# Sparse attention and a mixture of experts on one core: the first expert chunk of each batch in eight plain block products instead of seven

## The chip, the cores and the metric

One NeuronCore of a Trainium2 chip runs the whole program. The metric is the device time of one execution in microseconds (us), the median over runs. The engines are TensorE (PE in the profile; matmuls into PSUM), VectorE (DVE), ScalarE (ACT), GpSimd (POOL) and SyncE (SP, which only issues DMAs here). Each works through its own instruction list in order; semaphores connect them.

## The reference

Block-sparse attention over 4 batches, 8 heads, 768 positions and head size 64, followed by four experts whose outputs are mixed with given weights:

```
scores = where(mask, q @ k.T / 8, -1e9)     # mask: neighbours, first and last block of 32, 3 sampled blocks
attn = softmax(scores) @ v                  # x = attn of all heads side by side: [3072, 512]
p = domain_probs / (domain_probs.sum(-1) + 1e-9)
for e in range(4):
    out += p[:, e:e+1] * (relu(x @ w1[e]) @ w2[e])     # w1 [512, 1024], w2 [1024, 512]
```

All inputs and outputs are float32.

## The kernel before

**Attention.** Each batch has 16 units: 4 for the first and last row block, 12 for six groups of up to four row blocks, half of the heads each. A unit goes through `S` (scores into PSUM, then mask and row minimum on DVE at L266, exponential on ACT at L269), `T` (transposes on PE, copies on ACT at L280), `A` (times v on PE at L291, division on DVE) and `X` (transposes on PE, and a copy into `xr`, the batch's tokens as 512 x 768). For batch 0 a loop of 19 rounds does `S` of unit n, `X` of n-3, `A` of n-2 and `T` of n-1, with nothing else for PE to do. The attention of batches 1 to 3 is laid between the expert work of the batch before, by estimated times (`drive`).

**Experts.** A chunk is half of an expert's hidden layer, four tiles of 128; there are 8 chunks per batch. The first layer of a chunk is done in two halves `s`. For each, w1 is a 2 x 2 block matrix (output half, k half) and the tokens are a 2 x 2 block matrix b11, b12, b21, b22 (k half, token half g of 384 tokens). The kernel before multiplies them with seven products of sums of blocks (Winograd's form of Strassen's method), in the order 2, 1, 5, 6, 3, 7, 4. The sums of weight blocks are made on DVE (L456 to L461), those of token blocks in `conversion` (L407 to L418), and the products are combined on DVE and ACT (L522 to L536).

Every operand is written as a rounded part and a remainder. The rounded part is a cast on ACT (`wo` L464 for weights, `xo` L392 for tokens, `h` L480 for w2). The remainder is a subtraction on POOL (L465, L481) or, for tokens, on DVE or POOL (L393). One product is six matmuls of 384 columns (L502): two k tiles times three pairs of parts. ReLU and its split are L509 on ACT and L510 on DVE. The second layer (`second`, L550) does three matmuls of 512 columns per step into one of three `po` banks; after the last of the four tiles, DVE adds the bank, times the token's weight, into `oacc` (L565).

**Order of the work.** Nothing is reordered after the program is written: each engine gets its instructions in the order in which the code emits them. `experts` emits first-layer products and second-layer steps so that ten products stand ahead of a batch's first step. When the last product of a batch is emitted, 18 steps remain; behind every second step from there on, `convert` emits one more piece of the next batch's token conversion. Weights run ahead too: `operands` keeps seven weight blocks ready, and `split_w2` makes the next chunk's w2 tile once the old one is used up, then asks for another load (L444). PSUM holds two attention banks `s`, one `a`, one each of `v` and `w` for first-layer products, and three `po`.

**The token weights.** `token_weights` issues the load of `probs` on SP (L620) and right behind it four DVE instructions (L621 to L624) that divide by the sums. It is called in round 9 of batch 0's loop. In round 12 the first two token blocks, which need only the first token half, are converted.

Of the kernel before, what the change touches and what calls it, by code (L numbers as in the profile page):

```python
# [8 lines left out]
F32 = mybir.dt.float32  # L9
# [8 lines left out]
P = 128  # L18
# [5 lines left out]
def attention_moe_kernel(ctx: ExitStack, tc, qb, kb, vr, sampled, sampled_t, probs, w1, w2, out):  # L24
# [38 lines left out]
    def f32(ap):  # L63
        return ap.bitcast(F32)
# [322 lines left out]

    xo = {}

    def split(n, src, eng):  # L390
        o = xo[n] = (xp if n in (1, 2) else later["x"]).tile([P, 2, KH, HS], F32R, name=f"xo{n}")
        nc.scalar.copy(o[:, 0], src)  # L392
        eng.tensor_sub(o[:, 1], src, f32(o[:, 0]))  # L393

    def token_blocks(b):
        return [xr[b][:, k * KH:(k + 1) * KH, g * HS:(g + 1) * HS] for k in range(2) for g in range(2)]

    def conversion(b):


        b11, b12, b21, b22 = (xr[b][:, k * KH:(k + 1) * KH, g * HS:(g + 1) * HS]
                              for k in range(2) for g in range(2))
        split(2, b21, nc.gpsimd)
        yield
        split(1, b11, nc.vector)
        yield
        nc.vector.tensor_sub(b11, b12, b11)  # L407
        split(5, b11, nc.vector)
        yield
        nc.vector.tensor_sub(b11, b22, b11)  # L410
        split(6, b11, nc.vector)
        yield
        split(3, b22, nc.gpsimd)
        yield
        nc.vector.tensor_sub(b12, b22, b12)
        split(7, b12, nc.vector)
        yield
        nc.vector.tensor_sub(b21, b21, b11)  # L418
        split(4, b21, nc.gpsimd)
        xr.pop(b)  # L420
        yield

    pieces = {}

    def convert(b):
        if b in pieces:
# [13 lines left out]

    def load_w2(n):
        if n < B * NCH * FT:
            r2[n] = raw.tile([P, DM], F32, name="r2")
            nc.sync.dma_start(r2[n], w2[n // FT % NCH, n % FT])  # L444

    def operands():
        for b in range(B):
            for c in range(NCH):
                r, s1 = {}, {}
                for s, n in ORDER:  # L450
                    if n == 2:
# [10 lines left out]
                    src = {1: a11, 5: s1.get(s), 2: a12, 6: a11, 3: a12, 7: a21, 4: a22}[n]  # L462
                    o = wp.tile([P, 2, KH, P], F32R, name="wo", bufs=NWO)
                    nc.scalar.copy(o[:, 0], src)  # L464
                    nc.gpsimd.tensor_sub(o[:, 1], src, f32(o[:, 0]))  # L465
                    wo[b, c, s, n] = o
                    if n == 4:
                        load_w1(b * NCH + c + 1, s)
                    yield

# [3 lines left out]
    def split_w2(n):  # L474
        if n >= B * NCH * FT:
            return
        r = r2.pop(n)
        h = wp.tile([P, DM], F32R, name="h2")
        l = wp.tile([P, DM], F32R, name="l2")
        nc.scalar.copy(h, r)  # L480
        nc.gpsimd.tensor_sub(l, r, f32(h))  # L481
# [11 lines left out]

    def first(b, c, s, n):
        ps_m, cp, hp = later["m"], later["c"], later["h"]
        w, x = wo.pop((b, c, s, n)), xo[n]

        def product(ps, fresh):
            m = 0
# [6 lines left out]
        def finish(half, g, src):  # L506
# [3 lines left out]
            nc.vector.scalar_tensor_tensor(hl, src, 0.0, f32(hh), op0=ALU.max, op1=ALU.subtract)  # L510
            hs[c, 2 * s + half, g] = (hh, hl)

        if n in (5, 2, 3):
            v = ps_m.tile([P, HS], F32, name="v", bufs=1)
            product(v, True)
        else:
            if n == 1:
                W[s] = ps_m.tile([P, HS], F32, name="w", bufs=1)
            product(W[s], n == 1)
        if n == 2:  # L520
            pt[s] = cp.tile([P, HS], F32, name="p1", bufs=1)
            nc.scalar.copy(pt[s], v)  # L522
        elif n == 1:
            nc.vector.tensor_add(pt[s], W[s], pt[s])  # L524
            finish(0, 0, pt[s])
        elif n == 5:
            zt[s] = cp.tile([P, HS], F32, name="z1", bufs=2)
            nc.scalar.copy(zt[s], v)
        elif n == 6:
            ut[s] = cp.tile([P, HS], F32, name="u1", bufs=1)  # L530
            nc.vector.tensor_add(ut[s], W[s], zt[s])
        elif n == 3:
            nc.vector.tensor_add(ut[s], v, ut[s])
            finish(0, 1, ut[s])
        elif n == 7:
            nc.vector.tensor_add(zt[s], W[s], zt[s])  # L536
            finish(1, 1, zt[s])
        else:
            finish(1, 0, W[s])
# [27 lines left out]
            nc.sync.dma_start(out[tok * P:(tok + 1) * P, :], accs.pop(tok))  # L567


    TB = NCH * (len(ORDER) * T1 + KT * FT * T2)  # L570
    OFF = 10
    NH = (5, 3)

    def experts():

        L = len(ORDER)
        for b in range(B):
            one = [(c, s, n) for c in range(NCH) for s, n in ORDER]
            two = [(c, g, f, j) for c in range(NCH) for g in (1, 0) for f in range(FT)
                   for j in range(HS // P)]  # L580
            p = q = 0
            after_first = False
            while q < len(two):

                wait = after_first and p < len(one) and one[p][2] == 4 and q < ready(p)
                if wait or p >= min(len(one), (q * NCH * L + OFF * len(two)) / len(two)):
                    second(b, *two[q])
                    q += 1
                    after_first = False
# [27 lines left out]
    psum_e = const.tile([P, NT // P], F32, name="psum_e")  # L617

    def token_weights():
        nc.sync.dma_start(pr, probs)  # L620
        nc.vector.reduce_sum(psum_e, pr, axis=AX.X)  # L621
        nc.vector.tensor_scalar(psum_e, psum_e, 1e-9, None, op0=ALU.add)
        nc.vector.reciprocal(psum_e, psum_e)
# [6 lines left out]
    with ExitStack() as only:  # L630
# [13 lines left out]
        for n in range(N + 3):  # L644
# [6 lines left out]
            if 0 <= n - 1 < N:  # L651
                us[n - 1].T(0)
                us[n - 1].T(1)
            if n == 1:
                load_q(0, 1)
                load_v(0, 1)
                copy_k(0, 1)
# [4 lines left out]
                copy_k(0, t + 2)  # L662

            if n == N - 7:
                token_weights()
                for s in range(2):
                    load_w1(0, s)
                    load_w2(s)
            if n == N - 4:
                pieces[0] = conversion(0)  # L670
                convert(0)
                convert(0)
            if N - 5 <= n < N + 2:
                next(weights)
            if N - 4 <= n < N:
# [14 lines left out]
    later["h"] = ctx.enter_context(tc.tile_pool(name="hp", bufs=2 * FT))  # L690
    later["c"] = ctx.enter_context(tc.tile_pool(name="cp", bufs=2))
    later["o"] = ctx.enter_context(tc.tile_pool(name="op", bufs=KT))
    convert(0)
    LEAD, TAIL = 12.0, 25.0
    for b in range(1, B):
# [77 lines left out]
```

## Time and profile before

| | us |
|---|---|
| median of 3 runs | 1327.17 (1326.28 to 1329.41) |
| profiled execution, its own time | 1327.28 |
| its span, first to last instruction | 1325.6 |
| TensorE matmul busy | 1257.2 (95%) |
| DVE, POOL, ACT busy | 763.7, 675.7, 638.2 |

The granted TensorE clock is 0.982 of full speed on average. One batch follows the next after about 319 us. A row of a timeline gives the start, the duration, engine and line, operation and tiles; in square brackets stand the idle time of that engine just before, and what ended it. PE time includes the pipeline, so the rate of matmuls is read from their starts.

### The profile page before, as it was taken

What the parts mean: (1) busy time and instruction counts of PE and PEld (TensorE: products, weight loads), DVE (VectorE), ACT (ScalarE), POOL (GpSimd) and SP (SyncE); (2) the same over time, 40 slices, a digit from 0 to 9 for tenths busy, and PEclk for the clock granted to TensorE, in tenths of its full rate; (3) what the DMA queues carried; (4) which work ended last, traced back from release to release, by engine and by line L of the source; (5) the groups of instructions that cost most, each with busy time, mean ns of one, the idle gap of its engine ahead of it and who ended that gap; (6) DMA issues with size and microseconds to landing.
All of it is one profiled execution on the core that took longest, in us unless ns stands there. A gap on an engine that the chain in (4) does not pass through costs nothing.

```text
span 1325.6 us, 31450 instructions
## 1 busy us (share of the span) xinstructions
PE 1257.2 (95%) x12238; PEld 1076.7 (81%) x12238; DVE 763.7 (58%) x1750; ACT 638.2 (48%) x1678; POOL 675.7 (51%) x872
## 2 busy tenths in 40 slices
PE   7677999999998999999999799999999989999998
PEld 4566888888887788888888688888888778888887
DVE  5476656556547666556555756556555565555553
ACT  4474455555544445555554444555554444444441
POOL 5544545555445455664644554565553464444451
PEclk9877999999999999999999999999999999999999
DMA  8833324544214233443525311443431222222211
GB/s 252 221 108 137 96 60 115 155 118 135 89 62 173 73 96 89 130 140 92 149 64 171 110 57 57 136 144 113 128 104 54 88 88 64 64 64 65 64 48 64
DMA packets 60050, 140.51 MB, mean 106 GB/s; under 512 B 7163, under 2 KB 8700, under 8 KB 59900
## 3 DMA queue, kind: packets, MB, share of 16 engines
q1 hardware_dynamic: 52816, 115.41, 28.0%
q0 software_dynamic: 7040, 23.07, 6.3%
q8 instruction: 96, 1.57, 0.5%
q14 instruction: 54, 0.44, 0.1%
q10 hardware_dynamic: 44, 0.00, 0.0%
HBM read 132.17 MB, written 6.29 MB: 104 GB/s over the span
## 4 chain that ended last, share of the span: by engine, by line
PE 84%; DVE 7%; ACT 3%; issue 2%; DMA 1%; POOL 1%; DVEq 0%; SPq 0%; ACTq 0%
PE po L550 37%; PE w L502 19%; PE v L502 14%; PE o L291 3%; PE tp L278 3%; PE s L256 2%; PE sw L325 2%; PE s L251 2%; DVE hl L510 2%; PE ow L356 1%; DVE xo L393 1%; ACT hh L509 1%; PE tw L346 1%; ACT xo L392 1%; DVE oacc L565 1%
## 5 line engine op out<-in xcount | busy, mean ns | idle before, releaser
L465 POOL TENSOR_TENSOR wo<-r,wo 128x256 fp32r<-128x256 f32 x384 | 298.9, 781 | 419.4 <-ACT wo L464 415.6
L502 PE MATMUL w<-xo,wo 128*128 128x384 f32 x1536 | 317.1, 342 | 13.1 <-DVE z L536 8.4
L550 PE MATMUL po<-h,hh 128*128 128x512 f32 x768 | 310.6, 404 | 13.6 <-DVE oacc L565 13.1
L502 PEld LDWEIGHTS w<-xo,wo 128*128 128x128 f32 x1536 | 275.8, 190 | 39.6 <-DVE z L536 9.7
L550 PE MATMUL po<-h,hl 128*128 128x512 f32 x768 | 304.9, 397 | 0.0
L550 PE MATMUL po<-l,hh 128*128 128x512 f32 x768 | 304.8, 397 | 0.0
L502 PE MATMUL v<-xo,wo 128*128 128x384 f32 x1152 | 237.6, 342 | 10.6 <-ACT p L522 7.9
L464 ACT CAST wo<-r 128x256 fp32r<-128x256 f32 x384 | 153.6, 400 | 185.7 <-DVE r L459 116.3
L502 PEld LDWEIGHTS v<-xo,wo 128*128 128x128 f32 x1152 | 206.6, 190 | 29.6 <-ACT p L522 9.2
L481 POOL TENSOR_TENSOR l<-r,h 128x512 fp32r<-128x512 f32 x128 | 168.1, 1314 | 44.7 <-ACT h L480 44.6
L550 PEld LDWEIGHTS po<-h,hh 128*128 128x128 f32 x768 | 144.8, 189 | 37.5 <-DVE oacc L565 17.2
L550 PEld LDWEIGHTS po<-h,hl 128*128 128x128 f32 x768 | 144.9, 189 | 33.9
L550 PEld LDWEIGHTS po<-l,hh 128*128 128x128 f32 x768 | 145.1, 189 | 15.2
L524 DVE TENSOR_TENSOR p<-w,p 128x384 f32<-128x384 f32 x64 | 35.7, 557 | 169.3 <-PE w L502 166.0
L565 DVE SCALAR_TENSOR_TENSOR oacc<-po,pr,oacc 128x512 f32<-128x512 f32 x168 | 120.0, 744 | 10.3 <-PE po L550 9.7
L269 ACT ACTIVATE p<-p,mx 128x256 f32<-128x256 f32 (+1 forms) x192 | 95.4, 498 | 51.9 <-DVE mx L266 51.9
L136 POOL DMA_INDIRECT v<-in_vr_dram,vidx x88 | 86.7, 985 | 54.4 <-PE o L291 23.3
L465 POOL TENSOR_TENSOR wo<-s,wo 128x256 fp32r<-128x256 f32 x64 | 48.5, 757 | 98.1 <-ACT wo L464 93.3
L266 DVE CUSTOM_DVE_ANT_1 p<-s,mask 128x256 f32<-128x256 f32 (+1 forms) x192 | 69.7, 417 | 39.9 <-PE s L256 39.4
L480 ACT CAST h<-r 128x512 fp32r<-128x512 f32 x128 | 79.1, 618 | 12.1 <-PE po L550 10.4
L509 ACT ACTIVATE hh<-p 128x384 fp32r<-128x384 f32 x64 | 33.6, 524 | 90.8 <-DVE p L524 90.7
L510 DVE SCALAR_TENSOR_TENSOR hl<-w,hh 128x384 fp32r<-128x384 f32 x64 | 35.7, 558 | 71.4 <-ACT hh L509 71.4
(113 smaller groups left out, 1472.1 us busy)
## 6 DMA issues: line engine op xcount, KB each, us to landing
r<-in_w_dram SPq DMA_DIRECT2D x64, 512.0 KB, 3.6
r<-in_w_dram SPq DMA_DIRECT2D x128, 256.0 KB, 2.6
v<-in_vr_dram SPq DMA_DIRECT2D x44, 384.0 KB, 5.4
k<-in_kb_dram SPq DMA_DIRECT2D x8, 768.0 KB, 6.2
out_dram<-oacc SPq DMA_DIRECT2D x24, 256.0 KB, 2.1
v<-in_vr_dram SPq DMA_DIRECT2D x44, 128.0 KB, 5.4
q<-in_qb_dram SPq DMA_DIRECT2D x20, 256.0 KB, 6.9
v<-in_vr_dram SPq DMA_DIRECT2D x4, 1024.0 KB, 10.0
```

What stands on the lines that cost most here:

```text
L136: nc.gpsimd.indirect_dma_start(out=v[:, i, 1], out_offset=None, in_=vr, element_offset=b * S * DM, in_offset=bass.IndirectOffsetOnAxis(ap= ...
L266: nc.vector.tensor_tensor_reduce(p.rearrange("p (a b) -> p a b", b=BLOCK), s[h][:n, i], mk, -SCALE, 3.0e38, ALU.add, ALU.min, mx[:n])
L269: nc.scalar.activation(p, p, AF.Exp, bias=mx[:n], scale=-1.0, accum_out=self.sums[:n, m:m + 1])
L464: nc.scalar.copy(o[:, 0], src)
L465: nc.gpsimd.tensor_sub(o[:, 1], src, f32(o[:, 0]))
L480: nc.scalar.copy(h, r)
L481: nc.gpsimd.tensor_sub(l, r, f32(h))
L502: nc.tensor.matmul(ps, w[:, wi, t], x[:, xi, t], start=fresh and m == 0, stop=m == 3 * KH - 1, skip_group_check=not fresh)
L509: nc.scalar.activation(hh, src, AF.Relu)
L510: nc.vector.scalar_tensor_tensor(hl, src, 0.0, f32(hh), op0=ALU.max, op1=ALU.subtract)
L550: nc.tensor.matmul(p, a[:, js], w, start=f == 0 and n == 0, stop=f == FT - 1 and n == 2)
L565: nc.vector.scalar_tensor_tensor(accs[tok], p, pe, accs[tok], op0=ALU.mult, op1=ALU.add)
```

## The change

1. For the first chunk of each batch (c = 0) the first layer is done in eight plain products per half: the output block (half, g) is w1(half, 0) times b(0, g) plus w1(half, 1) times b(1, g), both into the same PSUM bank, and is then finished by ReLU and split straight from that bank. The order of the eight output blocks is the table `FIRST`; the first three need only the first token half. The banks `v` and `w` alternate. The weights of that chunk are then the eight plain blocks, each used twice. Two weight blocks are made behind the fourth, fifth, seventh and eighth output block, none behind the others.
2. `conversion` makes the plain b12 and b22 first and the sums later, in twelve steps with a cast one step ahead of its remainder, and two more steps (the sum for product 7, into the buffer that held plain b12) behind product 15 of the first chunk.
3. Twelve products, not ten, stand ahead of a batch's first second-layer step. Chunks 1 to 7 are as before.
4. `probs` is loaded in round 3; the four DVE instructions stand in round 17, behind the last unit's `A`.
5. w2 has three raw buffers, and three loads are asked for at the start. The tile `z1` has one buffer, not two.

```diff
     def conversion(b):
-        split(2, b21, nc.gpsimd)
-        yield
-        split(1, b11, nc.vector)
-        yield
-        nc.vector.tensor_sub(b11, b12, b11)
-        split(5, b11, nc.vector)
...
+        def cast(n, src):
+            xo[n] = (xp if n in (1, 2) else later["x"]).tile([P, 2, KH, HS], F32R, name=f"xo{n}")
+            nc.scalar.copy(xo[n][:, 0], src)
+        def rest(n, src, eng):
+            eng.tensor_sub(xo[n][:, 1], src, f32(xo[n][:, 0]))
+        cast(2, b21)
+        yield
+        rest(2, b21, nc.gpsimd)
+        cast(1, b11)
+        yield
+        rest(1, b11, nc.vector)
+        yield
+        cast(7, b12)
+        yield
+        rest(7, b12, nc.vector)
+        cast(3, b22)
+        yield
+        rest(3, b22, nc.gpsimd)
         nc.vector.tensor_sub(b11, b12, b11)
-        split(5, b11, nc.vector)
-        yield
+        yield
+        cast(5, b11)
+        yield
+        rest(5, b11, nc.vector)
         nc.vector.tensor_sub(b11, b22, b11)
...
+        yield
+        cast(6, b11)
         nc.vector.tensor_sub(b12, b22, b12)
...
+        yield
+        rest(6, b11, nc.vector)
         nc.vector.tensor_sub(b21, b21, b11)
+        yield
+        cast(4, b21)
+        yield
+        rest(4, b21, nc.gpsimd)
+        yield
+        cast(7, b12)
+        yield
+        rest(7, b12, nc.vector)
         xr.pop(b)
+    EARLY, PLAIN = 3, 12
+    FIRST = [((0, 0, 0), 0), ((0, 1, 0), 0), ((1, 0, 0), 0), ((0, 0, 1), 2), ((0, 1, 1), 2),
+             ((1, 1, 0), 0), ((1, 0, 1), 2), ((1, 1, 1), 2)]
+    XOF = {(0, 0): 1, (1, 0): 2, (0, 1): 7, (1, 1): 3}
...
-            r2[n] = raw.tile([P, DM], F32, name="r2")
+            r2[n] = raw.tile([P, DM], F32, name="r2", bufs=3)
...
-        load_w2(n + 2)
+        load_w2(n + 3)
...
     def first(b, c, s, n):
+        if c == 0:
+            half, k, g = n
+            w, x = wo[b, c, s, (half, k)], xo[XOF[k, g]]
...
+        if c == 0:
+            i = [item for item, _ in FIRST].index((s, half, g))
+            if k == 0:
+                W[0] = ps_m.tile([P, HS], F32, name="vw"[i % 2], bufs=1)
+            product(W[0], k == 0)
+            if k == 1:
+                finish(half, g, W.pop(0))
+                for _ in range(FIRST[i][1]):
+                    next(weights, None)
+            return
...
-            zt[s] = cp.tile([P, HS], F32, name="z1", bufs=2)
+            zt[s] = cp.tile([P, HS], F32, name="z1", bufs=1)
...
-                    if p < L:
-                        convert(b)
+                    if p < 2 * L:
+                        convert(b, PLAIN if p <= L else PLAIN + 2)
...
     def token_weights():
-        nc.sync.dma_start(pr, probs)
...
+            if n == 3:
+                nc.sync.dma_start(pr, probs)
+            if n == N + 1:
+                token_weights()
...
             if n == N - 7:
-                token_weights()
                 for s in range(2):
                     load_w1(0, s)
-                    load_w2(s)
+                for f in range(3):
+                    load_w2(f)
             if n == N - 4:
                 pieces[0] = conversion(0)
-                convert(0)
-                convert(0)
+                for _ in range(EARLY):
+                    convert(0)
```

PE, where batch 0's expert work begins behind the last attention transposes. `xo` with a number is one token operand (before, 2028 is b21, 2031 b11, 2462 the first sum). Before:

```order
L310 MATMUL x<-ident,xg 128x64 x4
L502 MATMUL v<-xo_2028,wo 128x384 x6
L502 MATMUL w<-xo_2031,wo 128x384 x6
L502 MATMUL v<-xo_2462,wo 128x384 x6
L502 MATMUL w<-xo_2477,wo 128x384 x6
L502 MATMUL v<-xo_2492,wo 128x384 x6
```

With the change (2029 is b11, 2026 b21, 2458 the plain b12, 2461 the plain b22):

```order
L310 MATMUL x<-ident,xg 128x64 x4
L537 MATMUL v<-xo_2029,wo 128x384 x6
L537 MATMUL v<-xo_2026,wo 128x384 x6
L537 MATMUL w<-xo_2029,wo 128x384 x6
L537 MATMUL w<-xo_2026,wo 128x384 x6
L537 MATMUL v<-xo_2029,wo 128x384 x6
L537 MATMUL v<-xo_2026,wo 128x384 x6
L537 MATMUL w<-xo_2458,wo 128x384 x6
```

The first product that reads anything of the second token half was the third in the list; it is now the seventh.

DVE, between the last product of batch 0 and the first ReLU of batch 1 (`xo` rows are remainders, `xr` rows sums of token blocks, `hl` the split behind a ReLU). Before:

```order
L393 TENSOR_TENSOR xo_6459<-xr,xo_6459 128x768
L565 SCALAR_TENSOR_TENSOR oacc<-po,pr,oacc 128x512 x2
L407 TENSOR_TENSOR xr<-xr 128x2x384
L393 TENSOR_TENSOR xo_6473<-xr,xo_6473 128x768
L565 SCALAR_TENSOR_TENSOR oacc<-po,pr,oacc 128x512
L410 TENSOR_TENSOR xr<-xr 128x2x384
L393 TENSOR_TENSOR xo_6486<-xr,xo_6486 128x768
L415 TENSOR_TENSOR xr<-xr 128x2x384
L393 TENSOR_TENSOR xo_6513<-xr,xo_6513 128x768
L418 TENSOR_TENSOR xr<-xr 128x2x384
L565 SCALAR_TENSOR_TENSOR oacc<-po,pr,oacc 128x512 x3
L524 TENSOR_TENSOR p_6572<-w,p_6572 128x384
```

With the change:

```order
L610 SCALAR_TENSOR_TENSOR oacc<-po,pr,oacc 128x512 x2
L402 TENSOR_TENSOR xo_6425<-xr,xo_6425 128x768
L610 SCALAR_TENSOR_TENSOR oacc<-po,pr,oacc 128x512
L402 TENSOR_TENSOR xo_6447<-xr,xo_6447 128x768
L417 TENSOR_TENSOR xr<-xr 128x2x384
L402 TENSOR_TENSOR xo_6486<-xr,xo_6486 128x768
L422 TENSOR_TENSOR xr<-xr 128x2x384
L610 SCALAR_TENSOR_TENSOR oacc<-po,pr,oacc 128x512 x2
L425 TENSOR_TENSOR xr<-xr 128x2x384
L610 SCALAR_TENSOR_TENSOR oacc<-po,pr,oacc 128x512
L402 TENSOR_TENSOR xo_6512<-xr,xo_6512 128x768
L428 TENSOR_TENSOR xr<-xr 128x2x384
```

The same eight token instructions stand there, but two `oacc` additions now come ahead of the first remainder, and the last three are spread between the sums; next behind these rows is `hl`.

ACT at the same place, with the change (`xo` rows are casts of tokens, `h` rows casts of w2, `hh` rows ReLU):

```order
L399 CAST xo_6447<-xr 128x768
L509 CAST h_6457<-r_6231 128x512
L399 CAST xo_6464<-xr 128x768
L509 CAST h_6477<-r_6290 128x512
L399 CAST xo_6486<-xr 128x768
L509 CAST h_6494<-r_6334 128x512
L399 CAST xo_6512<-xr 128x768
L509 CAST h_6518<-r_6461 128x512
L399 CAST xo_6535<-xr 128x768
L544 ACTIVATE hh_6543<-v 128x384
L544 ACTIVATE hh_6561<-w 128x384
```

Casts of tokens and of w2 alternate, and the last token cast, which reads the last sum of DVE's list, stands ahead of the first ReLU.

More of the change, by code (lines that the diff above doesn't have):

```diff
@@ L388, in attention_moe_kernel @@
     xo = {}
[L390 to L396, printed above, removed]
     def conversion(b):
@@ L402, in conversion, with convert @@
                               for k in range(2) for g in range(2))
-        split(2, b21, nc.gpsimd)
+        def cast(n, src):
[4 more added lines that the diff above has]
+        cast(2, b21)
         yield
-        split(1, b11, nc.vector)
+        rest(2, b21, nc.gpsimd)
+        cast(1, b11)
         yield
+        rest(1, b11, nc.vector)
[6 more added lines that the diff above has]
+        rest(3, b22, nc.gpsimd)
         nc.vector.tensor_sub(b11, b12, b11)
-        split(5, b11, nc.vector)
         yield
+        cast(5, b11)
+        yield
+        rest(5, b11, nc.vector)
         nc.vector.tensor_sub(b11, b22, b11)
-        split(6, b11, nc.vector)
         yield
-        split(3, b22, nc.gpsimd)
+        cast(6, b11)
+        nc.vector.tensor_sub(b12, b22, b12)
         yield
-        nc.vector.tensor_sub(b12, b22, b12)
-        split(7, b12, nc.vector)
+        rest(6, b11, nc.vector)
+        nc.vector.tensor_sub(b21, b21, b11)
         yield
-        nc.vector.tensor_sub(b21, b21, b11)
-        split(4, b21, nc.gpsimd)
+        cast(4, b21)
[5 more added lines that the diff above has]
+        rest(7, b12, nc.vector)
         xr.pop(b)
         yield
+    EARLY, PLAIN = 3, 12
     pieces = {}
-    def convert(b):
-        if b in pieces:
+    steps = {}
+    def convert(b, limit=PLAIN):
+        if b in pieces and steps.get(b, 0) < limit:
+            steps[b] = steps.get(b, 0) + 1
             next(pieces[b], None)
     ORDER = [(s, n) for s in range(2) for n in (2, 1, 5, 6, 3, 7, 4)]
+    FIRST = [((0, 0, 0), 0), ((0, 1, 0), 0), ((1, 0, 0), 0), ((0, 0, 1), 2), ((0, 1, 1), 2),
+             ((1, 1, 0), 0), ((1, 0, 1), 2), ((1, 1, 1), 2)]
+    XOF = {(0, 0): 1, (1, 0): 2, (0, 1): 7, (1, 1): 3}
     wo = {}
@@ L449, in operands @@
                 r, s1 = {}, {}
-                for s, n in ORDER:
-                    if n == 2:
+                plain = [(s, (i, k)) for s in range(2) for i in range(2) for k in range(2)]
+                for s, n in ORDER if c else plain:
+                    if n in (2, (0, 0)):
                         r[s] = r1.pop((b, c, s))
@@ L495, in first @@
         ps_m, cp, hp = later["m"], later["c"], later["h"]
-        w, x = wo.pop((b, c, s, n)), xo[n]
+        if c == 0:
+            half, k, g = n
+            w, x = wo[b, c, s, (half, k)], xo[XOF[k, g]]
+            if g:
+                wo.pop((b, c, s, (half, k)))
+        else:
+            w, x = wo.pop((b, c, s, n)), xo[n]
         def product(ps, fresh):
@@ L577, in experts @@
         for b in range(B):
-            one = [(c, s, n) for c in range(NCH) for s, n in ORDER]
+            one = [(0, s, (half, k, g)) for (s, half, g), _ in FIRST for k in range(2)]
+            MORE = len(one) - L
+            one += [(c, s, n) for c in range(1, NCH) for s, n in ORDER]
             two = [(c, g, f, j) for c in range(NCH) for g in (1, 0) for f in range(FT)
@@ L583, in experts @@
             while q < len(two):
-                wait = after_first and p < len(one) and one[p][2] == 4 and q < ready(p)
-                if wait or p >= min(len(one), (q * NCH * L + OFF * len(two)) / len(two)):
+                wait = after_first and p < len(one) and one[p][2] == 4 and q < ready(p - MORE)
+                if wait or p >= min(len(one), (q * NCH * L + (OFF + MORE) * len(two)) / len(two)):
                     second(b, *two[q])
```

8 lines of the change are left out of this document (5 added, 3 removed).

## The prediction

> **What bounds the kernel now.** I read the busy shares of five stretches first, then the waits of PE in the joint between two batches, then timelines of single engines there.
>
> ```profile
> 20.00:98.00 78.00, 58.64 (x1708) 45.45 (x1706) 44.74 (x182) 50.01 (x161) 37.33 (x63) 0.85 0.59 165
> 98.00:124.00 26.00, 17.54 (x67) 15.76 (x68) 17.10 (x23) 11.18 (x23) 11.55 (x11) 0.74 0.53 187
> 124.00:410.00 286.00, 284.04 (x2947) 244.40 (x2946) 163.27 (x402) 145.27 (x394) 148.45 (x199) 1.00 0.36 110
> 410.00:443.00 33.00, 25.30 (x112) 20.63 (x111) 24.10 (x29) 14.02 (x28) 19.00 (x16) 0.95 0.35 112
> 729.00:763.00 34.00, 26.31 (x118) 22.03 (x117) 24.80 (x29) 14.50 (x29) 19.91 (x17) 0.95 0.33 108
> ```
>
> The columns are the stretch, its length, busy time of PE, weight loads, DVE, ACT and POOL, then the granted clock. Within a batch (third row) PE is busy for 284 of 286 us at full clock: there every product is paid in full and no wait is left to win. What can be won lies in batch 0's attention, in its hand-over to the experts (clock 0.74), and in the three joints (the fourth and fifth rows show two).
>
> **Part 1, the token weights.** At round 9 DVE stands for a small load:
>
> ```profile
> 66.26 0.25 DVE L621 TENSOR_REDUCE psum_e<-pr 128x24 f32<-128x96 f32 x1 [6.34 <-DMA pr<-in_probs_dram]
> 67.28 0.42 DVE L266 CUSTOM_DVE_ANT_1 p<-s,mask 128x256 f32<-128x256 f32 x1
> 58.91 1.16 PE L291 MATMUL o<-v,pt 128*32 128x64 f32 x64
> 60.00 1.09 PE L278 MATMUL tp<-ident,p 128*128 128x128 f32 x8
> 70.33 1.94 PE L291 MATMUL o<-v,pt 128*32 128x64 f32 x64 [8.10 <-ACT pt L280]
> 72.20 1.97 PE L278 MATMUL tp<-ident,p 128*128 128x128 f32 x8
> ```
>
> Behind that wait queue the score rows of DVE, behind those ACT's exponentials and `pt`, and behind those PE, idle for 8.10 us. The change takes away the wait, 6.34, and the four instructions, 67.28 - 66.26 = 1.02: 7.4 us. PE then also ran at half speed: the same 64 matmuls take 1.94 instead of 1.16, the eight transposes 1.97 instead of 1.09, and the scores behind them lose about as much again, an estimate of 2.3 us in all. What is late next is the first weight block, which ACT casts in order between exponentials:
>
> ```profile
> 75.74 0.40 ACT L464 CAST wo<-r 128x256 fp32r<-128x256 f32 x1
> 60.34 0.55 SPq L444 DMA_DIRECT2D r<-in_w_dram  x1
> r<-in_w_dram SPq DMA_DIRECT2D x1, 256.0 KB, 8.9
> ```
>
> That cast would come up at 75.74 - 9.7 = 66.0. Its block was issued between `probs`, which landed at 66.26, and the load of 60.34, which landed 8.9 us later, at 69.2. So ACT waits between 0.3 and 3.2 us, and I take 1.5. Part 1 gives 7.4 + 2.3 - 1.5 = **8.2 us**, between 5 (the latest landing, part of the slow clock kept) and 9.7 (no wait). The moved load is one 0.4 us issue more on SP in round 3, ahead of later attention loads that wait for PE anyway; nothing.
>
> **Part 2, batch 0's hand-over.**
>
> ```profile
> 98.42 1.31 PE L502 MATMUL v<-xo,wo 128*128 128x384 f32 x6 [0.52 <-DVE xr L312]
> 103.55 2.12 PE L502 MATMUL v<-xo,wo 128*128 128x384 f32 x6 [2.78 <-ACT p L522]
> 122.72 0.39 PE L550 MATMUL po<-h,hh 128*128 128x512 f32 x1
> 441.02 1.20 PE L502 MATMUL v<-xo,wo 128*128 128x384 f32 x6
> 442.05 0.40 PE L550 MATMUL po<-h,hh 128*128 128x512 f32 x1
> 442.75 1.20 PE L502 MATMUL w<-xo,wo 128*128 128x384 f32 x6
> ```
>
> The first product starts as soon as the last token copy is done, at 98.4. From there to the first second-layer step at 122.7 ten products take 24.3 us, though one costs 442.05 - 441.02 = 1.03 and a step 0.70. The change puts twelve there, 12.4 us if nothing waits. But the order of ACT and DVE puts conversions ahead of ReLUs, and POOL and DVE get in each other's way:
>
> ```profile
> 419.64 1.53 POOL L481 TENSOR_TENSOR l<-r,h 128x512 fp32r<-128x512 f32 x1 [7.85 <-ACT h L480]
> 421.12 2.57 POOL L393 TENSOR_TENSOR xo<-xr,xo 128x768 fp32r<-128x768 f32 x1
> 419.94 2.04 DVE L415 TENSOR_TENSOR xr<-xr 128x768 f32<-128x768 f32 x1
> 422.89 1.62 DVE L393 TENSOR_TENSOR xo<-xr,xo 128x768 fp32r<-128x768 f32 x1 [0.90 <-ACT xo L392]
> 415.69 0.96 DVE L393 TENSOR_TENSOR xo<-xr,xo 128x768 fp32r<-128x768 f32 x1 [0.90 <-ACT xo L392]
> 409.94 1.85 POOL L393 TENSOR_TENSOR xo<-xr,xo 128x768 fp32r<-128x768 f32 x1
> 409.03 1.57 ACT L392 CAST xo<-xr 128x768 fp32r<-128x768 f32 x2
> L510 DVE SCALAR_TENSOR_TENSOR hl<-p,hh 128x384 fp32r<-128x384 f32 x14 | 11.1, 792 | 8.3 <-ACT hh L509 8.3
> L510 DVE SCALAR_TENSOR_TENSOR hl<-w,hh 128x384 fp32r<-128x384 f32 x14 | 7.8, 558 | 17.1 <-ACT hh L509 17.1
> L509 ACT ACTIVATE hh<-w 128x384 fp32r<-128x384 f32 x14 | 6.9, 491 | 7.2 <-PE w L502 7.2
> ```
>
> A token subtraction takes 0.96 alone and 2.04 beside POOL, whose own grows from 1.85 to 2.57: they end one after the other, as if they took turns. The split from PSUM (`hl<-w`) stays at 0.56, and the plain chunk has only that kind. A cast is 0.8, a ReLU 0.5.
>
> From the token copy's end: casts of plain b12 and b22 to 0.85 and 1.6, remainder of b12 on DVE to 1.9, of b22 on POOL to 3.7, first sum on DVE to 4.6, its cast to 5.4, and only then the first ReLU to 5.85 and split to 6.45. The third output block needs bank `v` back and has been due at 4.4: 2.1 us lost. Then remainder, two sums and a cast hold the second ReLU to 9.6, its split to 10.2 (1.65 lost), and a remainder, a sum and the last cast the third, to 13.4 and 14.0 (1.65 lost). The rest is free: 18.2 us, plus 0.6 since the four token-weight instructions, about 1.0 us, now stand ahead of the last token copy, plus 1.7 for one stretch of slow clock: 20.5. Part 2 gives 24.3 - 20.5 = **3.8 us**, between 0.5 (two more slow stretches) and 11.1 (nothing waits: 13.2). The two products more are paid in this.
>
> **Part 3, the three joints.**
>
> ```profile
> 408.15 0.39 PE L550 MATMUL po<-h,hh 128*128 128x512 f32 x1
> 413.32 0.50 PE L550 MATMUL po<-h,hh 128*128 128x512 f32 x1 [0.82 <-DVE oacc L565]
> 417.36 0.50 PE L550 MATMUL po<-h,hh 128*128 128x512 f32 x1 [2.38 <-DVE oacc L565]
> 429.51 1.30 PE L502 MATMUL v<-xo,wo 128*128 128x384 f32 x6 [1.23 <-ACT p L522]
> 428.46 0.62 ACT L480 CAST h<-r 128x512 fp32r<-128x512 f32 x1 [0.59 <-DMA r<-in_w_dram]
> 412.53 1.40 DVE L565 SCALAR_TENSOR_TENSOR oacc<-po,pr,oacc 128x512 f32<-128x512 f32 x2
> 415.50:419.00 3.50, 1.64 (x5) 1.30 (x6) 2.48 (x3) 0.95 (x3) 0.00 (x0) 0.83 0.21 78
> 419.00:422.50 3.50, 3.50 (x12) 2.76 (x11) 2.92 (x2) 1.77 (x4) 2.86 (x2) 0.69 0.04 6
> ```
>
> From 408.15 to 442.05 the last 18 steps and the first ten products take 33.9 us; 18 x 0.70 + 10 x 1.03 = 22.9, so 11.0 are lost. The new order ends two `oacc` additions at 412.4, the first remainder at 413.4 and the third addition at 414.05, so the steps lose only 0.4 and end at 421.15. Meanwhile DVE does a remainder and a sum to 415.95. ACT's next token cast stands behind the cast of w2's second tile, which waits for PE until 416.95, and ends at 418.35. POOL is then in turn: its token remainder to 419.0, DVE's to 419.9, POOL's `l` to 421.15, DVE's second sum to 422.0. Two additions to 423.4, the third sum to 424.35, the last addition to 425.05. POOL's last `l` goes first, to 425.6; remainder to 426.5, last sum to 427.45; last token cast to 428.3, then ReLU and split to 429.35. The third output block has been due at 421.15 + 4 x 1.03 = 425.3: 4.1 us lost. Eight products more: 429.4 + 8 x 1.03, 0.3 for restarts and 1.7 of slow clock give 439.65. The cover by w2's third buffer takes the 0.59 us DMA wait away: its load is then asked for at 417.2 and used at 422.9. A joint gains 442.05 - 439.65 = **2.4 us**, two products included, between 0.3 (POOL always first: 441.7) and 8.3 (the chain hidden: 433.75).
>
> The slow clock: after the 2.38 us gap the two stretches quoted were granted 0.83 and 0.69. That is half speed for 0.34 x 3.5 + 0.62 x 3.5 = 3.4 us, which costs 1.7; the 1.23 us gap left the clock alone. [...]
>
> **The sum.** 1327.28 - 8.2 - 3.8 - 3 x 2.4 = 1308.1; the profiled execution lies 0.1 above the median of the runs. POOL's and ACT's savings (eight weight blocks instead of 14) are off the path, as PE's 284 of 286 shows. One buffer for `z1` costs nothing:
>
> ```profile
> L510 DVE SCALAR_TENSOR_TENSOR hl<-z,hh x3: 558/558/559, 289.7 to 331.3; 128x384 fp32r<-128x384 f32 x3
> L528 ACT COPY z<-v x2: 480/480/480, 301.3 to 321.1; 128x384 f32<-128x384 f32 x2
> ```
>
> The read that frees it starts at 289.7, and the next write at 301.3, 11 us later.
>
> **Rivals.**
>
> *Conversions leave the path.* For it: ReLUs are short and DVE is busy for only 24 of 33 us in the joint. Against: the order has the last sum and cast ahead of the first ReLU. All upper ends: 1327.3 - 9.7 - 11.1 - 3 x 8.3 = 1281.6; halfway from my forecast is 1295.
>
> *Short gaps cost no clock.* The new gaps of 2.1 and 4.1 us leave PE at full speed, as the one of 1.23 us did: four times 1.7 less, 1301. Against: the 2.38 us gap. [...]
>
> *Waits are handed on.* The weights land late, the hand-over has three slow stretches, POOL goes first in each joint: 1327.3 - 5 - 0.5 - 0.9 = 1321. For it: a load of 256 KB took 8.9 us at that place, and DVE and POOL, 24.1 and 19.0 us busy and taking turns, leave a joint of 33 us little slack.
>
> *Slower: the single `z1`.* If the copy of z (28 chunks x 2 halves) had to wait for DVE's split of the other half, it would hold bank `v`; with 0.5 us each, about what the copy itself lasts, 56 x 0.5 = 28 us against 19 won: 1336. It decides from the point where that split comes 11 us later than now; nothing quoted suggests it.
>
> **How the numbers follow.** Forecast 0.60 (own range 1303 to 1315), conversions off the path 0.17, clock 0.05, handed on 0.14, slower 0.04. The range 1296 to 1319 cuts the far ends of the second and fourth. About 0.2% (2.7 us) is what a measurement can tell: faster 0.94, same 0.02, slower 0.04.
>
> **What would show it.** Right: no DVE wait on `pr`; first products at about 90 us; in the joints no PE wait for `oacc` above 1 us, and one of some 4 us before the third output block, its bank freed by `hl`; expert rows in between unchanged. Wrong: a PE wait elsewhere within a batch, a long ACT wait for `r`, or a joint without the 4 us wait.

## The result, and the profile after

The changed kernel takes 1304.41 us (median of 4 runs, 1303.35 to 1305.68); the kernel before takes 1328.29 on the same chip (4 runs, 1326.28 to 1330.34). The ratio is 0.9825, with a 95% interval of 0.9812 to 0.9838: 23.9 us less. The prediction said 1308.1, with 1303 to 1315 for the case that it held likeliest and 1296 to 1319 over all its cases. The profiled execution took 1304.3 us, its span 1302.6.

The busy shares of two stretches of the changed kernel: batch 0's hand-over to the experts, and the first joint. The columns are those of the table before.

```profile
96.00:116.00 20.00, 15.31 (x82) 14.21 (x83) 12.69 (x16) 7.79 (x15) 6.58 (x6) 1.00 0.56 202
396.00:428.00 32.00, 28.67 (x134) 25.36 (x133) 17.12 (x23) 12.46 (x23) 15.97 (x12) 0.95 0.41 135
```

Two things differ at a glance. The hand-over runs at full clock (1.00, and 0.74 before), and DVE's load in a joint has fallen from 24.1 to 17.1 us. The joint has kept its 0.95.

PE's waits from 100 us to the end in the changed kernel, with the total, how many, and the longest:

```profile
PE v L537 <- DVE hl L545: 12.2, 5, 3.1
PE po L595 <- DVE oacc L610: 2.1, 6, 0.4
PE po L595 <- DVE oacc L608: 1.7, 3, 0.6
PE w L537 <- DVE hl L545: 1.3, 1, 1.3
```

The longest of the same list in the kernel before:

```profile
PE po L550 <- DVE oacc L565: 13.1, 9, 2.4
PE w L502 <- DVE z L536: 8.4, 7, 1.9
PE v L502 <- ACT p L522: 7.9, 4, 2.8
PE w L502 <- DVE u L531: 4.4, 3, 1.6
```

With 2.1 more for z and 0.5 for `oacc` it sums to 36.4 us. These 36.4 us became 17.3. Every wait that came from combining products (p, u, z) is gone: the plain chunk, which now stands where most of those waits were, has nothing to combine. One kind took their place, and the forecast named it: the ReLU's split `hl`, 3.1 us in each joint.

The 23.0 us by which the span shrank, stretch by stretch on the same chip:

| stretch | before | after | gain | forecast |
|---|---|---|---|---|
| batch 0, to the start of the last transposes | 97.57 | 94.90 | 2.7 | 8.2 |
| from there to the first second-layer step | 25.15 | 19.26 | 5.9 | 3.8 |
| three joints: last 18 steps and all products ahead of the next step | 3 x 33.9 | 3 x 30.6 | 9.9 | 7.2 |
| within batches 0 to 2 | 3 x 285.4 | 3 x 283.9 | 4.5 | 0 |
| within batch 3 | 244.9 | 244.9 | 0 | 0 |

The total came out 3.8 us better than the sum, and no term was exactly right. The attention gave much less, each of the others more.

**Batch 0's attention.** DVE no longer waits for `pr`. But PE got two waits that were not there:

```profile
63.08 0.40 PE L251 MATMUL s<-k,q 64*32 64x96 f32 x16 [3.13 <-issue]
64.22 1.09 PE L291 MATMUL o<-v,pt 128*32 128x64 f32 x63
69.39 0.26 PE L291 MATMUL o<-v,pt 128*32 128x64 f32 x1 [4.08 <-issue]
73.12 0.40 ACT L493 CAST wo<-r 128x256 fp32r<-128x256 f32 x1
```

"Issue" means that the engine waited for nothing the profile shows. 3.13 + 4.08 = 7.2 us stand in the place of the 8.10 us for `pt`. The second wait is odd: 63 of a unit's 64 matmuls are through, all of one kind, and the last comes 4 us later. ACT's first weight cast (73.12) waits for no load at all.

**The hand-over.** The starts of product pairs, and the first step:

```profile
96.35 2.37 PE L537 MATMUL v<-xo,wo 128*128 128x384 f32 x12 [1.12 <-DVE xr L312]
102.58 2.36 PE L537 MATMUL v<-xo,wo 128*128 128x384 f32 x12 [1.77 <-DVE hl L545]
106.28 2.35 PE L537 MATMUL w<-xo,wo 128*128 128x384 f32 x12 [1.34 <-DVE hl L545]
109.86 2.35 PE L537 MATMUL v<-xo,wo 128*128 128x384 f32 x12 [1.23 <-DVE hl L545]
114.16 0.40 PE L595 MATMUL po<-h,hh 128*128 128x512 f32 x1
```

The three gaps are where they were expected, in front of the third, fourth and fifth output block, with 1.77, 1.34 and 1.23 us of idle time. The forecast's 2.1, 1.65 and 1.65 count from start to start, and so counted the three blocks lost 2.07, 1.62 and 1.50 (the first is 102.58 - 96.35 less four products of 1.04). Each pair takes 2.4 us behind its gap: no slow clock.

**A joint.** The end of batch 0 and the start of batch 1, first PE and then DVE:

```profile
404.05 0.50 PE L595 MATMUL po<-h,hh 128*128 128x512 f32 x1 [0.28 <-DVE oacc L610]
411.15 2.27 PE L537 MATMUL v<-xo,wo 128*128 128x384 f32 x12
418.56 3.17 PE L537 MATMUL v<-xo,wo 128*128 128x384 f32 x12 [3.05 <-DVE hl L545]
421.53 3.04 PE L537 MATMUL w<-xo,wo 128*128 128x384 f32 x12
424.40 2.24 PE L537 MATMUL v<-xo,wo 128*128 128x384 f32 x12
428.59 0.39 PE L595 MATMUL po<-h,hh 128*128 128x512 f32 x1
```

```profile
413.75 0.74 DVE L610 SCALAR_TENSOR_TENSOR oacc<-po,pr,oacc 128x512 f32<-128x512 f32 x1
414.41 1.38 DVE L402 TENSOR_TENSOR xo<-xr,xo 128x768 fp32r<-128x768 f32 x1
415.71 0.94 DVE L428 TENSOR_TENSOR xr<-xr 128x768 f32<-128x768 f32 x1
417.94 0.56 DVE L545 SCALAR_TENSOR_TENSOR hl<-v,hh 128x384 fp32r<-128x384 f32 x1 [1.29 <-ACT hh L544]
```

The two large waits for `oacc` (0.82 and 2.38) have shrunk to 0.28. DVE works through the forecast chain in the forecast order: third sum, last addition, remainder, last sum, and only then the first `hl`, which frees the bank that PE has needed since 418.56 - 3.05 = 415.5. Behind the gap one pair takes 421.53 - 418.56 = 2.97 and the next 424.40 - 421.53 = 2.87 us, where a pair at full clock takes 2.08: 1.68 lost to the clock.

### The profile page after: what moved, and what is told of

Read it like the earlier page. It is cut to its first block, busy times and chain, and to the rows that moved or that the text cites. A ratio compares the mean times of both kernels' runs of the same rounds, so it can differ in the third digit from the quotient of the medians.

```text
span 1302.6 us, 31439 instructions
## 1 busy us (share of the span) xinstructions
PE 1252.1 (96%) x12286; PEld 1080.3 (83%) x12286; DVE 715.6 (55%) x1690; ACT 622.6 (48%) x1642; POOL 659.1 (51%) x848
## 3 DMA queue, kind: packets, MB, share of 16 engines
q8 instruction: 96, 1.57, 0.5%
## 4 chain that ended last, share of the span: by engine, by line
PE 90%; DVE 6%; issue 2%; ACT 2%; DVEq 0%; DMA 0%; ACTq 0%
PE po L595 40%; PE w L537 20%; PE v L537 15%; PE o L291 4%; PE tp L278 3%; PE s L256 2%; PE s L251 2%; PE sw L325 1%; DVE oacc L610 1%; DVE xo L402 1%; PE ow L356 1%; PE x L310 1%; DVE hl L545 1%; PE tw L346 1%; DVE xr L422 1%
## 5 line engine op out<-in xcount | busy, mean ns | idle before, releaser
L494 POOL TENSOR_TENSOR wo<-r,wo 128x256 fp32r<-128x256 f32 x368 | 288.8, 788 | 412.0 <-ACT wo L493 411.1
L537 PE MATMUL w<-xo,wo 128*128 128x384 f32 x1536 | 310.8, 339 | 1.3 <-DVE hl L545 1.3
L537 PE MATMUL v<-xo,wo 128*128 128x384 f32 x1200 | 244.3, 341 | 13.3 <-DVE hl L545 12.2
L537 PEld LDWEIGHTS v<-xo,wo 128*128 128x128 f32 x1200 | 217.3, 190 | 31.5 <-DVE hl L545 13.8
L493 ACT CAST wo<-r 128x256 fp32r<-128x256 f32 x368 | 146.7, 401 | 157.1 <-DVE r L487 97.7
L510 POOL TENSOR_TENSOR l<-r,h 128x512 fp32r<-128x512 f32 x128 | 171.2, 1338 | 41.9 <-ACT h L509 41.6
L569 DVE TENSOR_TENSOR p<-w,p 128x384 f32<-128x384 f32 x56 | 31.2, 558 | 161.6 <-PE w L537 161.6
L494 POOL TENSOR_TENSOR wo<-s,wo 128x256 fp32r<-128x256 f32 x56 | 41.2, 736 | 97.5 <-ACT wo L493 97.5
L545 DVE SCALAR_TENSOR_TENSOR hl<-w,hh 128x384 fp32r<-128x384 f32 x72 | 40.1, 557 | 75.4 <-ACT hh L544 75.4
L544 ACT ACTIVATE hh<-p 128x384 fp32r<-128x384 f32 x56 | 29.4, 525 | 91.7 <-DVE p L569 91.7
```

The source lines that it names most:

```text
L537: nc.tensor.matmul(ps, w[:, wi, t], x[:, xi, t], start=fresh and m == 0, stop=m == 3 * KH - 1, skip_group_check=not fresh)
```

## Experiments

They ran on two other chips, where the kernel before takes 1333 to 1335 us. Its attention is some 6 us longer there, with many PE waits of 0.4 to 1.9 us ahead of score matmuls. Ratios are to the kernel before on the same chip.

### One part alone, and all parts but one

The early probabilities alone, put into the kernel before. Theory A in these texts is that the wait is handed on to PE's waits on "issue" because of the weight loads; theory B is that those belong to the attention itself and the gain is kept:

```diff
     def token_weights():
-        nc.sync.dma_start(pr, probs)
...
+            if n == 3:
+                nc.sync.dma_start(pr, probs)
+            if n == N + 1:
+                token_weights()
...
             if n == N - 7:
-                token_weights()
```

> The kernel before with the token weights changed alone (load in round 3, sums in round 17). Theory A: the removed DVE wait of 7.4 us is handed on to TensorE, which in rounds 10 to 12 then stands in 'issue' waits of 3 to 4 us while the weight loads fill the DMA queues; the time falls by 2 to 3 us. Theory B (the prediction's part 1): the whole wait and the slow clock behind it are won and the small gain seen so far is due to something else in the change; the time falls by 7 to 9 us.

Measured: 1334.13 us, ratio 1.0001 (0.9989 to 1.0013). Nothing is gained. Both theories expected more than that, and theory A is the nearer.

The changed kernel without them, and with the two w2 buffers of before:

```diff
-            if n == 3:
-                nc.sync.dma_start(pr, probs)
-            if n == N + 1:
-                token_weights()
             if n == N - 7:
+                nc.sync.dma_start(pr, probs)
+                token_weights()
...
-            r2[n] = raw.tile([P, DM], F32, name="r2", bufs=3)
+            r2[n] = raw.tile([P, DM], F32, name="r2")
...
-        load_w2(n + 3)
+        load_w2(n + 2)
```

> The changed kernel with the old place of the token weights and two w2 buffers: the plain products and the new conversion order alone. Theory A: it keeps nearly everything, about 20 us faster than before (hand-over 5 to 6, joints 3 x 3.3, and 1 to 1.5 us per batch within the batches), so 2 to 4 us behind the full change. Theory B: it loses the 8 us of part 1 and is 15 us faster than before.

Measured: 1311.81 us, ratio 0.9828 (0.9806 to 0.985), as much as the whole change (0.9825) and a little more than theory A's 20 us. So the plain chunk with its order of conversions is the whole gain, as far as intervals of 0.2% tell.

The changed kernel with the first weight loads in round 3, not in round 9, away from the two PE waits:

```diff
             if n == 3:
                 nc.sync.dma_start(pr, probs)
+                for s in range(2):
+                    load_w1(0, s)
+                for f in range(3):
+                    load_w2(f)
...
-            if n == N - 7:
-                for s in range(2):
-                    load_w1(0, s)
-                for f in range(3):
-                    load_w2(f)
```

> The full change with batch 0's first loads of w1 and w2 asked for in round 3 instead of round 9, so that the DMA queues are not filled in rounds 9 to 11. Theory A: TensorE's 'issue' waits of 3.1 and 4.1 us between 59 and 70 us go or shrink below 1 us each, and the time falls by 5 to 7 us against the full change. Theory B: those waits belong to the attention's own loads or to TensorE's instruction supply as such; they stay, and the time stays within 1 us.

Measured: 1312.95 us, ratio 0.9838 (0.9818 to 0.9859). No gain, as theory B says. But the two waits that theory A names are not in this trace: no matmul with v (L291) waits on "issue", and "PE s L251 <- issue" sums to 10.8 us in 15 waits, most of them the short ones of this chip, the longest 1.9. So neither theory holds as a whole. The changed kernel itself was not run on this chip, so what its two waits would have been there is open.

The third w2 buffer and the single z1 alone, in the kernel before:

```diff
-            r2[n] = raw.tile([P, DM], F32, name="r2")
+            r2[n] = raw.tile([P, DM], F32, name="r2", bufs=3)
...
-        load_w2(n + 2)
+        load_w2(n + 3)
...
-            zt[s] = cp.tile([P, HS], F32, name="z1", bufs=2)
+            zt[s] = cp.tile([P, HS], F32, name="z1", bufs=1)
```

> The kernel before with three w2 buffers, three first loads, and one z1 buffer, alone. Prediction: the 0.59 us wait for a w2 load in each joint goes, less than 2 us in all, and the single z1 buffer costs nothing. Rival (waits on z1): slower by several us. Rival (the load wait holds ACT's queue for longer than its idle time shows): faster by 3 us or more, and the wait of bank v for ACT's copy of p in the joints, 1.23 us, goes.

Measured: 1338.85 us, ratio 1.0031 (1.0015 to 1.0046): 4.2 us slower, against the prediction and of the size that the rival of waits on z1 named. PE's waits for z were 10.4 us, where the first chip's kernel before has 8.4, which is half of it. To split the two edits, the single z1 alone was tried later:

> The kernel before with one buffer for z1 and not two, and nothing else. The kernel before with a third w2 buffer and one z1 buffer was slower by 0.15 to 0.46 per cent. If the single z1 costs that: 1.002 to 1.005 here, with PE's waits for z longer than the 8.4 us in all of the kernel before. If the third w2 buffer costs it: 0.999 to 1.001.

Measured: 1334.73 us, ratio 1.001 (0.9999 to 1.0021), with 9.0 us of waits for z. The time lies on the upper end of the second case, the interval reaches into the first, and the waits are longer, as the first says: it does not decide. The changed kernel has no PE wait for z at all.

### What PE waits for in the attention

The changed kernel and the kernel before were profiled once more, beside the next kernel, which adds DMA load that nobody uses.

> The changed kernel once more, beside the kernels sent with it, so that their profiles can be set against it on one chip: 0.982 to 0.984 of the kernel before. If its attention phase again has many PE waits on 'issue' of 0.4 to 1.9 us in the score matmuls (10 us in all), they belong to the chip; if it has a few of 2 to 4 us, they belong to the program.

> The kernel before, for its profile on this chip alone. Theory A (the early probabilities bring nothing because the wait is handed on): its last attention transposes end within 1.5 us of those of the changed kernel. Theory B (the wait is removed, and only the trace of the first chip hid it): 5 us or more later than in the changed kernel.

Measured: the changed kernel 1311.88 us, ratio 0.9836 (0.9806 to 0.9865); the kernel before 1333.54 in one run. The many short waits belong to the chip: both kernels have them here. The last transposes start at 103.76 before and at 103.33 after, 0.4 us apart, as theory A says. The round in question, first before, then after:

```profile
73.31 0.25 DVE L621 TENSOR_REDUCE psum_e<-pr 128x24 f32<-128x96 f32 x1 [6.47 <-DMA pr<-in_probs_dram]
77.38 1.14 PE L291 MATMUL o<-v,pt 128*32 128x64 f32 x64 [2.90 <-ACT pt L280]
```

```profile
78.76 0.22 PE L291 MATMUL o<-v,pt 128*32 128x64 f32 x1 [1.78 <-issue]
83.83 0.42 PE L291 MATMUL o<-v,pt 128*32 128x64 f32 x14 [1.21 <-issue]
86.34 0.86 PE L291 MATMUL o<-v,pt 128*32 128x64 f32 x42
87.40 0.54 PE L291 MATMUL o<-v,pt 128*32 128x64 f32 x22 [0.20 <-issue]
```

DVE's wait of 6.47 us cost PE 2.90 here. Without it PE goes on, and stops for 1.78, 1.21 and 0.20 instead, 3.2 in all. Count the matmuls from the second of these stops to the third: 14, then 8 transposes and 64 score matmuls, which are not shown, then 42. That makes 128, each with its weight load, so 256 instructions. On the first chip 127 matmuls lie between the two waits, one of them again behind the 63rd of 64. Two rows of the changed kernel's page answer to that:

```profile
PE 1252.1 (96%) x12286; PEld 1080.3 (83%) x12286; DVE 715.6 (55%) x1690; ACT 622.6 (48%) x1642; POOL 659.1 (51%) x848
q8 instruction: 96, 1.57, 0.5%
```

The DMA queue of kind "instruction" moved 96 packets of 1.57 MB / 96 = 16.4 KB, and PE's 2 x 12286 matmuls and weight loads make 96 blocks of 256. The reading that fits all of this is that PE stops where one block of its own instruction list ends and the next has not come.

The trace has the times of these packets, and they bear it out. On the first chip the changed kernel's eight stops on "issue" in the attention come behind 449, 705, 961, 1217, 1729, 1985, 2241 and 2497 instructions of PE (matmuls, weight loads and, up to the last stop, 18 of its sequencer), whole multiples of 256 apart, and each ends 1.3 to 1.6 us after a packet of this queue has landed. For the two stops above the packets landed at 61.76 and 67.81, and PE went on at 63.08 and 69.39. In the kernel before, the packet of the last of these blocks landed at 66.12, inside the 8.10 us in which PE stood for `pt`, and cost nothing.

The load was then raised in the same rounds:

```diff
+            if N - 9 <= n < N - 3:
+                nc.sync.dma_start(extra, w1[0, 0])
             if n == N - 7:
```

> The changed kernel with six extra loads of 512 KB each into a tile that nobody reads, one in each attention round from the ninth before the last to the fourth before the last. Theory E (PE's waits on 'issue' in the attention phase come from a loaded DMA: the program's loads and PE's own instruction packets share the same engines): they grow by 3 us or more in all, and the last attention transposes end 3 us or more later. Rival F (they do not hang on the DMA load): both stay within 1 us.

Measured: 1316.51 us, ratio 0.9878 (0.9852 to 0.9904), 4.6 us more than the changed kernel beside it. In it the same stops:

```profile
78.64 0.22 PE L291 MATMUL o<-v,pt 128*32 128x64 f32 x1 [1.82 <-issue]
85.36 0.65 PE L291 MATMUL o<-v,pt 128*32 128x64 f32 x14 [2.85 <-issue]
```

They come at the same two matmuls; one is unchanged, the other grew from 1.21 to 2.85, and the transposes start 2.5 us later (105.84 and 103.33). Both figures miss the 3 us of theory E, and both are outside the 1 us of theory F. From 70 to 85 us the DMA engines were busy for a share of 0.74 in the changed kernel and of 0.98 with the extra loads, from 85 to 95 us for 0.09 and 0.38. In the changed kernel on the first chip the start of the next packet goes with this share: it begins 1.1 to 1.8 us after PE has gone on behind one of the eight stops where the share in between is 0.00 to 0.81, and 3.4 to 4.9 us after where it is 0.96 to 1.05. So the packet started later where the DMA engines were loaded, and that this made the one stop grow is the author's reading; when a packet was asked for is not on record. The short waits of 0.4 to 1.2 us ahead of single score matmuls on these chips follow each other within a few matmuls (0.52, 0.52 and 1.12 us from 66.89 to 69.09 in the changed kernel), so they are not 256 instructions apart, and have no cause found.

### The conversions off the path

```diff
-                    if p < 2 * L:
+                    if p == 0:
+                        convert(b, 6)
+                    elif 9 <= p < 2 * L:
                         convert(b, PLAIN if p <= L else PLAIN + 2)
```

From step 7 on the conversion makes the operands of products 5, 6 and 4, which only the second chunk needs. What is left of it when a batch's first product is emitted (steps 7 to 12 in batch 0; steps 10 to 12 in the joints, where nine are emitted behind second-layer steps) now stands behind the ninth product.

> The changed kernel with the conversion steps from the seventh on (blocks 5, 6, 4 and the second block 7) put off until the tenth product of the batch, so that VectorE has only the ReLU chain beside the plain products. Theory C (the 3.1 us PE wait for hl before the third output block, and the slow clock behind it, come from conversions queued ahead of the ReLU on VectorE): no PE wait for hl over 1 us in the joints, granted clock 1.00 there, each joint 4 to 5 us shorter, the first batch's hand-over 17.8 to about 13.5 us; in all 15 to 20 us less than the changed kernel. Rival D (the work is only moved): the first products of the second chunk wait for xo of blocks 5 and 6, 2 to 4 us in each batch, and the gain is 5 to 10 us.

Measured: 1294.94 us, ratio 0.9717 (0.9692 to 0.9742), 17.0 us less than the changed kernel. The joint of the changed kernel on that chip, and of this one:

```profile
419.64 2.27 PE L537 MATMUL v<-xo,wo 128*128 128x384 f32 x12
427.05 4.21 PE L537 MATMUL v<-xo,wo 128*128 128x384 f32 x12 [3.06 <-DVE hl L545]
438.12 0.39 PE L595 MATMUL po<-h,hh 128*128 128x512 f32 x1
```

```profile
413.99 2.27 PE L537 MATMUL v<-xo,wo 128*128 128x384 f32 x12
426.52 0.39 PE L595 MATMUL po<-h,hh 128*128 128x512 f32 x1
417.25 0.55 DVE L545 SCALAR_TENSOR_TENSOR hl<-v,hh 128x384 fp32r<-128x384 f32 x1
```

From the first product to the first step it is 12.5 us for 18.5: twelve products at 1.04. The first `hl` comes 3.3 us behind the first product, ahead of the conversions that were put off. Its busy shares from 412 to 428 us, and all that is left of PE's waits from 115 us to the end:

```profile
412.00:428.00 16.00, 16.00 (x90) 15.46 (x89) 11.49 (x15) 6.00 (x13) 9.26 (x7) 1.00 0.41 135
PE po L595 <- DVE oacc L610: 2.1, 6, 0.4
PE po L595 <- DVE oacc L608: 1.7, 3, 0.6
PE w L537 <- DVE hl L545: 0.5, 1, 0.5
```

No wait for `xo` appears, so rival D falls; theory C holds in the joints (5.9 us in the one shown, whose pairs behind the gap lost the most to the clock, 2.73 us; 4.9 and 4.7 in the others, against 4 to 5), in the clock (1.00 in the first of these rows) and in the total. Only the hand-over gained less, from 17.8 to 14.2 us, not 13.5. The next runs show why.

### What the other edits are worth in that kernel

Three versions side by side: the same kernel again, one with the token weights where they were, one with two w2 buffers. Their edits are those shown above.

> The changed kernel with its conversions put off to the tenth product, once more, beside two kernels that undo one part of it each: 0.971 to 0.973 of the kernel before; no PE wait for hl over 1 us after the first batch.

> The same, with the probabilities loaded and summed where the kernel before does it. If removing VectorE's wait for them is worth its 6 us, this is 5 to 8 us slower than the kernel beside it; if the wait is only handed on to the score matmuls (as in the attention phase of the kernel with the early probabilities alone), within 2 us.

> The same, with two w2 blocks in flight and not three (loads two blocks ahead, two first loads). If the third buffer still hides something, 0.6 us in each joint or 1 to 3 us slower in all; if it hides nothing here, within 1 us.

Measured: 1294.84 us (ratio 0.9704, 0.9687 to 0.9721), 1293.47 (0.9697, 0.9682 to 0.9712) and 1295.25 (0.9709, 0.9692 to 0.9725). All three are the same within their intervals, as expected of a wait that is only handed on and of a buffer that hides nothing. The probabilities' place and the third w2 buffer are worth nothing that can be measured, also where the joints are clean. The hand-over of the first and the second of them:

```profile
104.57 3.87 PE L537 MATMUL v<-xo,wo 128*128 128x384 f32 x12 [1.12 <-DVE xr L312]
118.75 0.39 PE L595 MATMUL po<-h,hh 128*128 128x512 f32 x1
```

```profile
103.59 2.37 PE L537 MATMUL v<-xo,wo 128*128 128x384 f32 x12 [0.52 <-DVE xr L312]
116.89 0.39 PE L595 MATMUL po<-h,hh 128*128 128x512 f32 x1
```

With the four sums ahead of the last token copy, PE waits 1.12 us for it, not 0.52, and the first pair then takes 3.87, not 2.37: 14.2 us, not 13.3. The early sums pay back there part of what they spare earlier. That the clock falls behind this wait is no rule: on the first chip the pair behind the same 1.12 us took 2.37. Of all the kernels run, these three with the late conversions are the fastest, 3% below the kernel before and some 17 us below the change.

## Why the prediction was right, and where not

**What bounds the kernel.** Joints, hand-over and attention were the right places. But "within a batch no wait is left to win" was wrong by 4.5 us. Its own row, 284.04 busy of 286, left 2 us, and these are the waits behind it, before and then after:

```profile
PE po L550 <- DVE oacc L565: 1.2, 1, 1.2
PE w L502 <- DVE z L536: 0.6, 1, 0.6
```

```profile
PE po L595 <- DVE oacc L608: 0.4, 1, 0.4
PE po L595 <- DVE oacc L610: 0.4, 1, 0.4
```

1.8 us in two waits became 0.8 in two, 1.0 of the 1.5 us in each of batches 0 to 2; batch 3 gained nothing. Why the shifted order spares them was not tried.

**Part 1** was mis-sized: 8.2 forecast, 2.7 measured, and nothing as an edit alone (1.0001) on another chip. The step that failed is "the change takes away the wait, 6.34, and the four instructions: 7.4 us". The wait did go, but PE could not use the time: it stopped on "issue" instead, 7.2 us for 8.10 on the first chip, 3.2 for 2.90 on the third, at places 256 instructions apart; at the two on the first chip it went on 1.3 and 1.6 us after an instruction packet had landed. The forecast did ask what is late next, and answered with the first weight block (1.5 us); ACT waited for no block. In the kernel before, the profile already had PE waits on "issue" in the attention (5.4 us in three of them ahead of score matmuls, the longest 4.3), and they were not asked what they are.

**Part 2** was right in its mechanism and low in its size: 5.9 for 3.8. The conversions did hold up the third, fourth and fifth output block in that order, for 2.07 + 1.62 + 1.50 = 5.2 us from start to start, where 5.4 were forecast, and the last token copy came 0.6 us later, as worked out. The term at fault is the 1.7 for one slow stretch, which fell away. From the first product to the first step it is then 17.8 us for the 18.2 worked out without that stretch; 0.2 of this difference lies in the gaps, the rest was not itemised.

**Part 3** was right in its mechanism and low in its size: 3.3 for 2.4 in each joint. The term at fault is the loss before the third output block, 3.25 us from start to start (3.05 of idle time) for 4.1: the first `hl` ended 7.35 us behind the first product (418.50 - 411.15), where 8.2 were worked out (429.35 - 421.15). The slow clock behind it was right: 1.68 for 1.7. The steps waited 0.28 us for `oacc` and lost about 0.5 in all, for 0.4.

**The rivals.** That the conversions leave the path did not happen in this change; made to happen in an experiment, it gave 17.0 us, and not the 26.5 us below the forecast at which all its upper ends were priced, since the attention's term and the hand-over's were out of reach. Short gaps that cost no clock: true in the hand-over on the first chip, false in all three joints. Waits handed on: true of Part 1 alone, and by another mechanism than the one named (weights landing late). The single z1 costs PE no wait in the changed kernel, as said; what it costs the kernel before stayed open.

**The signs.** Of those named as right, the DVE wait on `pr` and the waits for `oacc` above 1 us are gone, and the wait before the third output block stands in every joint. The first product starts at 96.35, though, not at about 90, and that was the sign that Part 1 had failed. The expert rows in between were to be unchanged, and got 1.5 us shorter in each of batches 0 to 2.

## What to carry to other kernels

A wait that is removed pays only as far as the next limit on that engine (here 7.2 us on "issue" came for the 8.10 us behind `pt`); when the profile shows waits on "issue" beside it, price them as a limit of their own before counting the gain. When a new order leaves an engine's queue full of work that is needed later, ask which entry in that queue frees a bank that PE needs now: moving three to six conversion steps behind nine products was worth 17 us, nearly as much as the change itself. And small edits that ride along with a large one want a run each: here the plain chunk with its order did all the work that could be measured.

## What the runs showed of the hardware

PE waited for its own instructions, by the reading above. In the attention of the changed kernel 128 matmuls and their weight loads go by in 3.6 us (83.83 to 87.40 above), and PE stops for 0.2 to 4.1 us at places 256 instructions apart, also in the middle of a run of 64 equal matmuls (69.39 and 78.76). On the first chip it went on 1.3 to 1.6 us after a packet of 16.4 KB of the queue of kind "instruction" had landed, at all eight stops. The next packet began 1.1 to 1.8 us after PE had gone on where the DMA engines' share was 0.00 to 0.81, and 3.4 to 4.9 us after where it was 0.96 to 1.05.

The clock fell for whole stretches of a grid. In both traces of the first chip, of the kernel before and of the changed kernel, the granted clock of PE is 1 or 0.5 and changes at times that lie whole multiples of 3.41 us apart. Two such stretches at the joint shown of the changed kernel, with the columns of the table before:

```profile
416.43:419.85 3.42, 1.29 (x7) 1.30 (x8) 1.25 (x3) 1.60 (x3) 1.83 (x1) 1.00 0.50 158
419.85:423.26 3.41, 3.41 (x13) 3.41 (x12) 0.56 (x1) 0.49 (x1) 0.00 (x0) 0.50 0.02 5
```

PE was idle for 2.1 us of the first, and ran the whole of the second at half speed, and the two pairs lost 1.68 us; the gap itself had ended at 418.56. In the two other joints on that chip the stretch before the slow one held 2.7 and 3.1 us of idle time. Stretches of products with 0.9 and 1.6 us of idle time (from 413.02 and 98.99) were followed by full clock. The stop of 3.13 us on "issue" lay with 1.5 us in one stretch and 1.6 us in the next (from 58.03 and 61.45), and full clock followed; the gap of 3.05 us in the joint lay with 0.9 and 2.1 us in two, and half speed followed. Of these two, about as long, the one that the grid split evenly cost no clock. Behind gaps of 3.05 to 3.08 us the next two pairs lost 1.5 to 2.9 us in all twelve joints of four runs, 1.7 in those of the changed kernel on the first chip, and 2.73 in the joint shown of the third, where the granted clock from 418 to 440 us was 0.84. The gap of 1.12 us ahead of the first product cost 1.5 on the third chip (3.75 us from the start of this pair to the next in the changed kernel, for 2.22 on the first) and nothing on the first, so a gap's length alone does not settle it.
